# An attention-and-MLP block on one Trainium2 core: jumps over the general path moved to the ends of the instruction queues, and the first loads reordered

## Chip, cores, metric

One core of a Trainium2 chip runs the whole program. The metric is the device time of one execution in microseconds (us).

Names used below: PE is TensorE, DVE is VectorE, ACT is ScalarE, POOL is GpSimd, SP is SyncE, which in this kernel issues nearly all loads. A load's issue is the time that the engine spends on handing it to the DMA engines; it lands when the data have arrived. In listings "SPq" is SP's queue of DMA issues and "PEclk" the TensorE clock that the chip granted, as a share of full speed.

## The reference, cut to what matters

```python
mod = (silu(c) @ w_mod)                      # 6 blocks of 640: sa, ca, ga, sb, cb, gb
h = layernorm(x) * (1 + ca) + sa             # x: 2048 x 640
q = h @ wq                                   # 32 heads of 128
p = softmax(q @ k_cache.T * 128 ** -0.5)     # 2048 x 2048 for each head
x = x + ga * ((p @ v_cache) @ wo)
... # second half: layernorm, two small matrices with gelu and shifts, an MLP of 1728
```

The kernel goes through the heads in groups of four and through the 2048 query rows in four chunks of 512. A "step" is one head of one chunk. Step 0 is head 0 of chunk 0, steps 1 to 3 are heads 1 to 3 of chunk 0, and step 4 is head 0 of chunk 1. So in the first 50 us the kernel has to fetch the modulation weights, the query weights and the keys and values of four heads, while it already computes.

## The kernel before

The kernel records its operations with priorities; a list scheduler then fixes the order on each engine's queue. The general path, code that the usual input does not take, lies in the program between two parts of each queue. `FIRST` says after how many operations each engine jumps over it, and `HINT` where it announces the jump.

```python
    ENG = ("PE", "ACT", "DVE", "POOL", "SP")
    FIRST = {"PE": 3, "ACT": 10000, "DVE": 0, "POOL": 7, "SP": -5}
    HINT = {"PE": 0, "ACT": -30, "DVE": 0, "POOL": 0, "SP": -12}
    ...
        for e, eng in names.items():
            n = self.HINT[e] % len(self.seq[e])
            run(e, 0, n)
            hint = eng.mark_branch_hint_location()
            run(e, n, self.FIRST[e])
            eng.br("fast").branch_hint(hint)
        es.close()
        general()
        nc.switch_bb("fast")
        for e, eng in names.items():
            run(e, self.FIRST[e], None)
```

The loads of the start. A number such as -296 is a priority, lower is earlier; `gate` makes a load wait for an earlier one; `need=from_slot(n)` holds it until the softmax of slot n has run. Keys are loaded with a transposing DMA in four chunks of 512 keys, and only SP issues those.

```python
    def load_k(h, prio, gate=(), need=()):
        b = h % NKV
        for i in range(4):
            dmaT(lambda e, i=i: e.dma_start_transpose(K_ap[b][:, i * 512:(i + 1) * 512]..., A_k_cache[0, h, i * 512:(i + 1) * 512, :]),
                 128, gate if i or h else (), (K[b][i],), prio + 0.01 * i, need)

    load_wq(0, 0, 1, -297)                                # query weights of head 0
    load_k(0, -296, gate=(wm[2],))
    ln1(0, -280)                                          # layernorm of chunk 0
    ...
    dma("ACT", lambda e: e.dma_start(pre_ap, mod_src(2)), 800, (wm[1],), pre_t, -292)   # modulation block 2, 800 KB
    ...
    load_v(0, -290, "ACT", gate=(wm[1],))                 # head 0's values, 512 KB

    def load_head(h):
        first = step_of(h // HG, 0, h % HG)
        pr = (first - 12) * NP if h >= HG else -310 + 20 * h
        n = first * NP - 14 if h < HG else (first - 12) * NP
        load_k(h, pr, (wm[2],) if h == 1 else (), from_slot(n))
        load_v(h, pr + 1, gate=(wm[2],) if h == 1 else (), need=from_slot(n + 1))
    ...
    load_wq(0, 1, HG, -295.985, gate=(wm[2],))            # query weights of heads 1 to 3, 480 KB
```

Chunk 1's rows are normalised on DVE and then turned by four transposing DMAs, also issued by SP; DVE applies the modulation to the result. That gives `hT` of chunk 1, which step 4 needs.

Of the kernel before, what the change touches and what calls it, by code (L numbers as in the profile page):

```python
# [6 lines left out]
ACT = mybir.ActivationFunctionType  # L7
# [33 lines left out]
class Plan:  # L41
# [1 line left out]


    ENG = ("PE", "ACT", "DVE", "POOL", "SP")
    FIRST = {"PE": 3, "ACT": 10000, "DVE": 0, "POOL": 7, "SP": -5}
    HINT = {"PE": 0, "ACT": -30, "DVE": 0, "POOL": 0, "SP": -12}

    def __init__(self):
        self.ops = []  # L50
# [113 lines left out]
    def emit(self, nc, es, ndma, redo, flag, general):  # L164
# [82 lines left out]
# [6 lines that stand above are left out]
# [3 lines left out]
        for e, eng in names.items():  # L256
            run(e, self.FIRST[e], None)
            eng.wait_ge(self.flag_op.sem, self.flag_op.semval)
# [7 lines left out]
def fast_path(nc, es, flag, A_x, A_k_cache, A_v_cache, A_wq, A_wo, B_w1, B_w2, B_w3, B_w4, c, w_mod, out):  # L266
# [9 lines left out]
    HG = 4  # L276
# [57 lines left out]
    K = [[T() for _ in range(4)] for _ in range(NKV)]  # L334
# [14 lines left out]
    hT = [[T() for _ in range(KT)] for _ in range(NC)]  # L349
# [11 lines left out]
    xn = [T(t[:]) for t in xn_t]  # L361
# [18 lines left out]
    from_slot = lambda n: () if n < 0 else (lambda: exps[n],)  # L380

    def dma(eng, fn, kb, reads, writes, prio, need=(), after=()):
        return P.op(eng, fn, {"SP": 480, "ACT": 480, "POOL": 1000}[eng], reads, writes, prio, dma=True, kb=kb, need=need, after=after)
# [31 lines left out]
    wm = [T() for _ in range(KT)]  # L415
# [38 lines left out]
    saT, caT = T(small(KT)), T(small(KT))  # L454
# [9 lines left out]
    mvs = [[T() for _ in range(4)] for _ in range(NMV)]  # L464
    rs_ap = [small(4) for _ in range(NMV)]
    rs = [T() for _ in range(NMV)]
# [45 lines left out]
    def normed(dst, dst_t, src, src_t, g, i, fp, prio):  # L512
        P.op("DVE", lambda e: e.tensor_scalar(out=dst, in0=src, scalar1=mv_ap[g][:, i, 0:1], scalar2=rs_ap[g][:, i:i + 1],
                                              op0=ALU.subtract, op1=ALU.mult),
             430 if fp else 240, (src_t, mvs[g][i], rs[g]), (dst_t,), prio)

    COST = {"POOL": (1600, 950), "DVE": (825, 430)}

    def tt(eng, out, a, b, op, rd, wr, prio):
        P.op(eng, lambda e: e.tensor_tensor(out=out, in0=a, in1=b, op=op), COST[eng][0], rd, wr, prio, lat=300 if eng == "POOL" else None)  # L520
# [11 lines left out]
                 (src_t, rs[g], mvs[g][i]), (out_t,), prio)  # L532


    XP, XS = (0, -294, -20, -20), (0, -1, 22, 44)

    def ln1(ch, prio):
        g = ln_slot()
        xs = x0 if ch == 0 else load_x2(4 * ch, XP[ch], from_slot(XS[ch])) + load_x2(4 * ch + 2, XP[ch], from_slot(XS[ch]))
        for a, z in ((0, 2), (2, 4)) if ch < 2 else ((0, 4),):  # L540
            for i in range(a, z):
                ln_stats(xs[i].ap, (xs[i],), g, i, prio, 0.0 if ch == 0 else 2000.0)
            if ch == 0:
                rstd_act(g, a, z, prio - 100)
            else:
                rstd_dve(g, a, z, prio - 1)
            for i in range(a, z):
                normed(xn[i].ap, xn[i], xs[i].ap, xs[i], g, i, False, prio - 1)
        raw = [T() for _ in range(4)]
        if ch == 0:  # L550
            hq = Tile(pool="S0")
            hp = [Tile(pool="O0"), Tile(pool="O1"), hq, hq, Tile(pool="M")]

            def hslice(k, i0, i1):
                return hp[k].ap.bitcast(BF16)[:, (1024 if k == 3 else 0) + i0 * 128:(1024 if k == 3 else 0) + i1 * 128]
            for i in range(4):
                def tr(e, i=i):
                    for k in range(KT):
                        ins = e.transpose(hslice(k, i, i + 1), xn[i][:, k * 128:(k + 1) * 128], ident_t[:])
                    return ins  # L560
                P.op("PE", tr, 330, (xn[i], ident), (hp[0], hp[1], hq, hp[4]), (-286.6 if i < 2 else -280) + 0.1 * i, accum=True)
            for k in (0, 2, 4, 1, 3):
                if k % 2:
                    P.op("ACT", lambda e, k=k: e.activation(hT_t[0][:, k, :], hslice(k, 0, 4), ACT.Identity,
                                                            scale=caT[:, k:k + 1], bias=saT[:, k:k + 1]),
                         770, (hp[k], saT, caT), (hT[0][k],), -280 + k)
                else:
                    P.op("DVE", lambda e, k=k: e.tensor_scalar(out=hT_t[0][:, k, :], in0=hslice(k, 0, 4), scalar1=caT[:, k:k + 1],  # L568
                                                               scalar2=saT[:, k:k + 1], op0=ALU.mult, op1=ALU.add),
                         540, (hp[k], saT, caT), (hT[0][k],), -280 + k)  # L570
        else:
            for i in range(4):
                dmaT(lambda e, i=i: e.dma_start_transpose(hT_t[ch][:, :, i * 128:(i + 1) * 128], xn[i].ap), 160, (xn[i],), (raw[i],), prio - 400)  # L573
            for k in range(KT):
                P.op("DVE", lambda e, k=k: e.tensor_scalar(out=hT_t[ch][:, k, :], in0=hT_t[ch][:, k, :], scalar1=caT[:, k:k + 1],  # L575
                                                           scalar2=saT[:, k:k + 1], op0=ALU.mult, op1=ALU.add),
                     210, tuple(raw) + (saT, caT), (hT[ch][k],), prio)


    def load_k(h, prio, gate=(), need=()):  # L580
        b = h % NKV
        for i in range(4):
            dmaT(lambda e, i=i: e.dma_start_transpose(K_ap[b][:, i * 512:(i + 1) * 512].unsqueeze(1), A_k_cache[0, h, i * 512:(i + 1) * 512, :]),
                 128, gate if i or h else (), (K[b][i],), prio + 0.01 * i, need)

    def load_v(h, prio, eng="SP", gate=(), need=()):
        b = h % NKV
        dma(eng, lambda e: e.dma_start(V_ap[b][:, :, 0:128], A_v_cache[0, h].rearrange("(t p) d -> p t d", p=128)), 512, gate, (V[b],), prio, need)

    def load_wq(g, a, b, prio, need=(), gate=()):  # L590
        dma("SP", lambda e: e.dma_start(wq_t[g % 2][:, :, a * 128:b * 128],
                                        A_wq[:, (g * HG + a) * 128:(g * HG + b) * 128].rearrange("(k p) d -> p k d", p=128)),
            160 * (b - a), gate, tuple(wq[g % 2][a:b]), prio, need)
# [4 lines left out]

    step_of = lambda g, ch, hh: (g * NC + ch) * HG + hh
    of_step = lambda s: (s // (NC * HG), s // HG % NC, s % HG)  # L600
    load_wq(0, 0, 1, -297)
    load_k(0, -296, gate=(wm[2],))
    ln1(0, -280)


    def modulation(p, hf, w_ap, w_t, pool, key, prio):
        m = Tile(pool=pool)
        sl = slice(hf * HD, (hf + 1) * HD)
        for k in range(KT):
            P.op("PE", lambda e, k=k: e.matmul(m[:, 0:HD], s_bc[:, k, :], w_ap[:, k, sl], start=(k == 0), stop=(k == KT - 1)),  # L610
                 MM(HD), (s_bc,) + w_t, (m,), key(k), accum=True)
        P.op("DVE", lambda e: e.tensor_scalar_add(out=mod[p][hf].ap, in0=m[:, 0:HD], scalar1=1.0 if p == 4 else 0.0),
             490, (m,), (mod[p][hf],), prio)

    mod_src = lambda p: w_mod[:, p * D:(p + 1) * D].rearrange("(k p) n -> p k n", p=128)
    pre_ap = KV_t[:, (NKV - 1) * KVW:(NKV - 1) * KVW + KT * D].rearrange("p (k n) -> p k n", k=KT)
    pre_t = tuple(K[NKV - 1]) + (V[NKV - 1],)
    dma("ACT", lambda e: e.dma_start(pre_ap, mod_src(2)), 800, (wm[1],), pre_t, -292)
    for hf in range(2):
        modulation(2, hf, pre_ap, pre_t, "O%d" % hf, lambda k, hf=hf: (-262, 0.5)[hf] + 0.01 * k, -50)  # L620
    v_ones(NKV - 1)
    load_v(0, -290, "ACT", gate=(wm[1],))

    def load_head(h):
        first = step_of(h // HG, 0, h % HG)
        pr = (first - 12) * NP if h >= HG else -310 + 20 * h
        n = first * NP - 14 if h < HG else (first - 12) * NP
        load_k(h, pr, (wm[2],) if h == 1 else (), from_slot(n))
        load_v(h, pr + 1, gate=(wm[2],) if h == 1 else (), need=from_slot(n + 1))

    def load_group(g):
        if g:
            load_wq(g, 0, HG, (step_of(g, 0, 0) - 8) * NP, from_slot((step_of(g, 0, 0) - 8) * NP))
        load_wo(g, (step_of(g, 0, 0) - 2) * NP, from_slot((step_of(g, 0, 0) + 1) * NP + 12 * (g == 0)))

    load_wq(0, 1, HG, -295.985, gate=(wm[2],))
    for h in range(1, NKV):
        load_head(h)
    load_group(0)
# [3 lines left out]
    for n, p in enumerate((4, 3, 5)):  # L643
        dma("SP", lambda e, n=n, p=p: e.dma_start(w_half[n % 2], mod_src(p)), 800, (), (W12[n % 2],) + (w2b if n == 1 else ()) + tuple(wm),
            MS * NP - 30 + n, from_slot((MS + 2 * n) * NP - 20))
        for hf in range(2):
            modulation(p, hf, w_half[n % 2], (W12[n % 2],) + (w2b if n == 1 else ()), "M",
                       lambda k, i=2 * n + hf: NP * (MS + i) + 4.65 + k, NP * MS - 60)

    TAIL = ("A0 B0 B1 A1 B2 B3 WO B4 B5 I3 A2 B6 C0 B7 D0 D1 D2 B8 D3 B9 C1 D4 A3 B10 B11 "  # L650
            "B12 D5 B13 D6 B14 D7 B15 C2 D8 D9 D10 D11 C3 D12 D13 D14 D15").split()
    WOKEY = 3000 + 50 * TAIL.index("WO")
    QUAD = (2, 3)
    WOD, CH, I3D = -100, -1000, -200


    evac, last_ot = [], []
# [156 lines left out]
    for s in range(NS):  # L814
# [3 lines left out]
        g, ch, hh = of_step(s)  # L818
# [138 lines left out]
    pr = 3400  # L957
# [762 lines left out]
```

## Time and profile before

| | before |
|---|---|
| median of 3 runs | 1390.7 us (1390.07 to 1392.28) |
| span of the profiled run | 1391.3 us |
| PE busy | 1379.4 us, 99% |
| ACT, DVE busy | 79%, 39% |

The first lines of the page of the kernel before: engines with busy time and share, and in the last line the chain of waits that ended last, by engine.

```profile
span 1391.3 us, 29861 instructions
PE 1379.4 (99%) x13128; PEld 941.2 (68%) x13128; DVE 539.6 (39%) x1401; ACT 1101.5 (79%) x1143; POOL 100.9 (7%) x88
...
PE 97%; DVE 1%; DMA 1%; SPq 0%; issue 0%; ACT 0%
```

PE is the limit; the change touches no arithmetic, so it can only win or lose PE's few gaps. These are the gaps of the start, from PE's timeline of the kernel before (start, duration, engine, line, operation, output<-inputs, size, count, and in brackets the idle time before it and what ended it):

```profile
11.74 0.29 PE L448 MATMUL f_M<-f_s_bf,f_W 128*128 128x1 bf16 x6
13.38 0.25 PE L448 MATMUL f_M<-f_s_bf,f_W 128*128 128x1 bf16 x4 [1.34 <-issue]
...
14.85 2.34 PE L666 MATMUL f_M<-f_hT,f_wq 128*128 128x512 bf16 x5 [0.64 <-DVE f_hT L568]
...
45.55 1.25 PE L666 MATMUL f_M<-f_hT,f_wq 128*128 128x512 bf16 x4 [0.26 <-DVE f_hT L575]
46.64 0.59 PE L734 MATMUL f_S<-f_PQ,f_KV 128*128 128x512 bf16 x2
49.17 0.61 PE L753 MATMUL f_O<-f_KV,f_PQ 128*128 128x129 bf16 x8 [1.94 <-DMA f_KV<-in_A_v_cache_dram]
```

Three things are to be seen. A group of ten small matmuls is cut in two by 1.34 us in which PE waits for nothing that is recorded ("issue"). The first query projection (line 666) takes 2.34 us for five matmuls, where the one at 45.55 takes 1.25 for four: it ran at about half clock (PEclk was 0.50 from 14.48 to 17.89). And at 49.17 PE waits 1.94 us for the values of head 3.

SP's queue in the same run says when the loads went out. A duration here is the time that SP spent on the issues, not the transfer:

```profile
10.70 0.58 SPq L591 DMA_DIRECT2D f_wq<-in_A_wq_dram  x1
11.32 4.52 SPq L583 DMA_TRANSPOSE f_KV<-in_A_k_cache_dram  x2
...
36.99 6.01 SPq L573 DMA_TRANSPOSE f_hT<-f_xn  x4
43.04 1.26 SPq L583 DMA_TRANSPOSE f_KV<-in_A_k_cache_dram  x1
44.35 0.58 SPq L588 DMA_DIRECT2D f_KV<-in_A_v_cache_dram  x1
```

Line 591 is the query weights of heads 1 to 3, line 573 the transposes of chunk 1, the last line head 3's values. When each load landed is read from the last of the events that raise its semaphore: the query weights at 19.17, chunk 1's last transpose at 44.41, head 3's values at 49.04. One key load of head 0, taken alone from the same queue, matters later:

```profile
9.53 1.12 SPq L583 DMA_TRANSPOSE f_KV<-in_A_k_cache_dram  x1
```

### The profile page before, as it was taken

Reading aid. Unit: us, or ns where it says so; the run is one execution under the profiler, and the core shown is the slowest. Engines: PE = TensorE matmul, PEld = TensorE weight load, DVE = VectorE, ACT = ScalarE, POOL = GpSimd, SP = SyncE. Lnnn points to the kernel's source line nnn. Section 1 sums busy time; section 2 is a strip of 40 time slices with the busy share of each in tenths; the row PEclk is TensorE's granted clock in tenths of the full one; section 3 lists DMA queues with packets and bytes.
Section 4 is the critical chain, followed back from the end, with each engine's and each line's share of the span. In section 5 each row is a group of like instructions: output and inputs, shape, how many; then the busy total and the mean of one; then the engine's idle time right before and its main releaser. Section 6 shows DMA issues by size and latency. Waiting matters only on the chain.

```text
span 1391.3 us, 29861 instructions
## 1 busy us (share of the span) xinstructions
PE 1379.4 (99%) x13128; PEld 941.2 (68%) x13128; DVE 539.6 (39%) x1401; ACT 1101.5 (79%) x1143; POOL 100.9 (7%) x88
## 2 busy tenths in 40 slices
PE   9999999999999999999999999999999999999999
PEld 6667767777777777777777776777776766645554
DVE  5453232333233322333233323332333245987553
ACT  5888888888888898888888888888888888732222
POOL 0000000000000000000000000000333248200000
PEclk9999999999999999999999999999999999999999
DMA  9651623161214221241205122612254102531210
GB/s 220 130 115 31 117 78 83 36 107 35 46 36 84 58 46 36 48 92 30 54 17 98 31 45 36 107 36 46 55 91 114 17 16 48 120 53 24 53 43 25
DMA packets 259179, 88.90 MB, mean 64 GB/s; under 512 B 236705, under 2 KB 257762, under 8 KB 259042
## 3 DMA queue, kind: packets, MB, share of 16 engines
q1 hardware_dynamic: 255762, 84.59, 30.7%
q10 hardware_dynamic: 3280, 2.33, 0.7%
q8 instruction: 105, 1.72, 0.5%
q14 instruction: 32, 0.26, 0.1%
HBM read 43.48 MB, written 2.62 MB: 33 GB/s over the span
## 4 chain that ended last, share of the span: by engine, by line
PE 97%; DVE 1%; DMA 1%; SPq 0%; issue 0%; ACT 0%
PE f_O L753 33%; PE f_S L734 31%; PE f_M L666 10%; PE f_M L691 10%; PE f_M L928 3%; PE f_S L914 2%; PE f_O L914 2%; PE f_S L928 2%; PE f_S L887 1%; PE f_S L864 1%; PE f_O L864 1%; PE f_M L887 1%; DMA f_W<-in_w_mod_dram 0%; DMA f_KV<-in_A_v_cache_dram 0%; SPq L573 0%; PE f_M L610 0%
## 5 line engine op out<-in xcount | busy, mean ns | idle before, releaser
L736 ACT ACTIVATE f_PQ<-f_S 128x1024 bf16<-128x1024 f32 x1024 | 1041.0, 1023 | 148.2 <-PE f_S L734 135.1
L753 PEld LDWEIGHTS f_O<-f_KV,f_PQ 128*128 128x128 bf16 x8192 | 589.4, 98 | 233.7 <-issue 2.4
L734 PE MATMUL f_S<-f_PQ,f_KV 128*128 128x512 bf16 x2048 | 726.9, 379 | 0.2 <-ACT f_PQ L736 0.2
L753 PE MATMUL f_O<-f_KV,f_PQ 128*128 128x129 bf16 x8192 | 713.0, 220 | 2.7 <-DMA f_KV<-in_A_v_cache_dram 1.9
L699 DVE TENSOR_TENSOR f_y<-f_M,f_y 128x320 f32<-128x320 f32 x192 | 94.3, 491 | 536.3 <-PE f_M L691 536.3
L691 PE MATMUL f_M<-f_wo,f_OO 128*128 128x320 bf16 x992 | 272.9, 299 | 0.0
L734 PEld LDWEIGHTS f_S<-f_PQ,f_KV 128*128 128x128 bf16 x2048 | 196.7, 97 | 30.5 <-ACT f_PQ L736 1.2
L666 PE MATMUL f_M<-f_hT,f_wq 128*128 128x512 bf16 x640 | 177.3, 381 | 1.1 <-DVE f_hT L568 0.6
L691 PEld LDWEIGHTS f_M<-f_wo,f_OO 128*128 128x128 bf16 x992 | 96.1, 98 | 28.5
L762 DVE TENSOR_TENSOR f_OO<-f_O,f_rl 128x256 bf16<-128x256 f32 x256 | 108.4, 423 | 8.1
L669 DVE CAST f_PQ<-f_M 128x512 bf16<-128x512 f32 x128 | 88.5, 691 | 56.9 <-PE f_M L666 56.8
L520 POOL TENSOR_TENSOR f_y<-f_y,f_mod 128x640 f32<-128x640 f32 x32 | 49.6, 1560 | 820.1 <-DVE f_y L699 819.9
L666 PEld LDWEIGHTS f_M<-f_hT,f_wq 128*128 128x128 bf16 x640 | 62.2, 98 | 65.9 <-DVE f_hT L575 1.5
L760 DVE RECIPROCAL f_rl<-f_O 128x2 f32<-128x2 f32 x256 | 43.4, 169 | 32.1 <-PE f_O L753 27.9
L928 PE MATMUL f_M<-f_KV,f_OO 128*128 128x320 bf16 (+1 forms) x308 | 47.1, 300 | 0.0
L917 ACT ACTIVATE f_OO<-f_O 128x512 bf16<-128x512 f32 (+1 forms) x28 | 16.6, 596 | 38.5 <-PE f_O L914 38.5
L526 ACT ACTIVATE f_xn<-f_y,f_small 128x640 bf16<-128x640 f32 x10 | 9.1, 915 | 41.6 <-DVE f_small L505 41.6
L928 PEld LDWEIGHTS f_M<-f_KV,f_OO 128*128 128x128 bf16 (+1 forms) x308 | 28.6, 97 | 18.7 <-issue 7.0
L697 DVE COPY f_y<-f_M 128x320 f32<-128x320 f32 x32 | 15.7, 490 | 63.5 <-PE f_M L691 63.5
L481 DVE BATCH_NORM_STATS2 f_small<-f_y 128x6 f32<-128x320 f32 x64 | 29.6, 480 | 2.0 <-POOL f_y L520 2.0
L917 ACT ACTIVATE f_OO<-f_S 128x512 bf16<-128x512 f32 (+1 forms) x28 | 16.7, 595 | 13.1 <-PE f_S L914 13.1
L942 DVE TENSOR_TENSOR f_y<-f_M,f_y 128x640 f32<-128x640 f32 x10 | 8.2, 825 | 43.2 <-PE f_M L928 43.2
(134 smaller groups left out, 513.9 us busy)
## 6 DMA issues: line engine op xcount, KB each, us to landing
f_KV<-in_A_v_cache_dram SPq DMA_DIRECT2D x31, 512.0 KB, 4.8
f_wo<-in_A_wo_dram SPq DMA_DIRECT2D x8, 640.0 KB, 4.4
f_xin<-in_A_x_dram SPq DMA_DIRECT2D x15, 320.0 KB, 4.6
f_wq<-in_A_wq_dram SPq DMA_DIRECT2D x7, 640.0 KB, 4.6
f_W<-in_w_mod_dram SPq DMA_DIRECT2D x3, 800.0 KB, 4.9
out_dram<-f_xin SPq DMA_DIRECT2D x15, 160.0 KB, 1.8
f_KV<-in_B_w_dram SPq DMA_DIRECT2D x5, 432.0 KB, 3.3
f_KV<-in_A_k_cache_dram SPq DMA_TRANSPOSE x128, 2.7
```

The costliest lines, as they stand in the source:

```text
L520: P.op(eng, lambda e: e.tensor_tensor(out=out, in0=a, in1=b, op=op), COST[eng][0], rd, wr, prio, lat=300 if eng == "POOL" else None)
L666: P.op("PE", lambda e, i=i, kk=kk: e.matmul(m.ap, wq_t[g % 2][:, kk, hh * 128:(hh + 1) * 128], hT_t[ch][:, kk, :], start=(i == 0), stop=(i ...
L669: P.op("DVE", lambda e: e.tensor_copy(q.ap, m.ap), 690, (m,), (q,), s * NP - 90)
L691: P.op("PE", lambda e, m=m, qt=qt, hf=hf, hh=hh: e.matmul(m[:, 0:HD], OT_ap[gs][:, qt, hh, :], wo_t[g % 2][:, hh, hf * HD:(hf + 1) * HD], ...
L699: P.op("DVE", lambda e, m=m, yt=yt: e.tensor_tensor(out=yt.ap, in0=m[:, 0:HD], in1=yt.ap, op=ALU.add), 490, (m, yt), (yt,), s * NP - 60)
L734: P.op("PE", lambda e, sp=sp, r=r, kt=kt: e.matmul(sp[:, r * QC:(r + 1) * QC], K_ap[b][:, kt * 128:(kt + 1) * 128], q.ap, start=True, stop ...
L736: x = P.op("ACT", lambda e, sp=sp, pt=pt: e.activation(pt.ap.rearrange("p k q -> p (k q)"), sp.ap, ACT.Exp, scale=SCALE), 1021, (sp,), (pt ...
L753: ins = e.matmul(o[bk][:, w * 129:w * 129 + 129], pt[:, r, qt * 128:(qt + 1) * 128], V_ap[b][:, u, 0:129], start=(u == 0 and w == 0), stop ...
L760: P.op("DVE", lambda e, ov=ov, i0=i0: e.reciprocal(rl_t[:, i0:i0 + 2].unsqueeze(2), ov[:, 0:258].rearrange("p (u d) -> p u d", u=2)[:, :, ...
L762: evac.append(P.op("DVE", lambda e, ov=ov, i0=i0, bk=bk: e.tensor_tensor(out=On_ap[gs][:, 2 * bk:2 * bk + 2, hh, :], in0=ov[:, 0:258].rear ...
L914: P.op("PE", lambda e, m=m, f=f, kk=kk, fs=fs: e.matmul(m[0:fs, :], w3_ap[:, kk, f * 128:f * 128 + fs], nT_ap[ch][:, kk, :], start=(kk == ...
L928: P.op("PE", lambda e, f=f, hf=hf, fs=fs: e.matmul(m[:, hf * 512:hf * 512 + HD], gT_ap[0:fs, f, i * 128:(i + 1) * 128], w4_ap[f][0:fs, hf ...
```

## The change

Read from the diff, the change aims at PE's gap at 12 us, by letting no engine jump early, and at PE's wait for head 3's values, by loading the values of heads 1 to 3 in one batch.

```diff
-    FIRST = {"PE": 3, "ACT": 10000, "DVE": 0, "POOL": 7, "SP": -5}
-    HINT = {"PE": 0, "ACT": -30, "DVE": 0, "POOL": 0, "SP": -12}
+    FIRST = {"PE": 100000, "ACT": 100000, "DVE": -6, "POOL": 100000, "SP": -5}
+    HINT = {"PE": -300, "ACT": -30, "DVE": -60, "POOL": -1, "SP": -12}
 ... (four cost estimates of the scheduler, and a later priority for normalising chunk 0)
-    XP, XS = (0, -294, -20, -20), (0, -1, 22, 44)
+    XP, XS = (0, -294.5, -20, -20), (0, -1, 22, 44)
 ... in load_k
-                 128, gate if i or h else (), (K[b][i],), prio + 0.01 * i, need)
+                 128, gate if i or h else (), (K[b][i],), prio + (1.6 if h == 0 and i else 0) + 0.01 * i, need)
 ...
-    load_wq(0, 0, 1, -297)
-    load_k(0, -296, gate=(wm[2],))
+    load_wq(0, 0, 1, -298)
+    load_k(0, -297.5, gate=(wm[2],))
 ...
-    dma("ACT", lambda e: e.dma_start(pre_ap, mod_src(2)), 800, (wm[1],), pre_t, -292)
+    dma("SP", lambda e: e.dma_start(pre_ap, mod_src(2)), 800, (wm[2],), pre_t, -297)
     for hf in range(2):
-        modulation(2, hf, ..., lambda k, hf=hf: (-262, 0.5)[hf] + 0.01 * k, -50)
+        modulation(2, hf, ..., lambda k, hf=hf: 0.5 + hf + 0.01 * k, -50)
-    load_v(0, -290, "ACT", gate=(wm[1],))
+    load_v(0, -296.5, gate=(wm[2],))
 ... in load_head
+        if h in (1, 2, 3):
+            load_k(h, (-294, -290, -289)[h - 1], (wm[2],), () if h < 3 else from_slot(n))
+            load_v(h, (-293, -291, -290.5)[h - 1], gate=(wm[2],))
+            return
 ...
-    load_wq(0, 1, HG, -295.985, gate=(wm[2],))
+    load_wq(0, 1, HG, -295.5, gate=(wm[2],))
 ... (order of the tail: B9 before D3, A3 before D4; WOD -200, I3D 100)
```

In effect: PE's and POOL's jumps come at the end and DVE's before its last six operations; modulation block 2 and head 0's values are issued by SP, not by ACT; the query weights of heads 1 to 3 go behind all of head 0's keys; the values of heads 1 to 3 go in one batch before head 2's keys.

More of the change, by code (lines that the diff above doesn't have):

```diff
@@ L514, in normed @@
                                               op0=ALU.subtract, op1=ALU.mult),
-             430 if fp else 240, (src_t, mvs[g][i], rs[g]), (dst_t,), prio)
-    COST = {"POOL": (1600, 950), "DVE": (825, 430)}
+             445, (src_t, mvs[g][i], rs[g]), (dst_t,), prio)
+    COST = {"POOL": (1600, 950), "DVE": (825, 590)}
     def tt(eng, out, a, b, op, rd, wr, prio):
@@ L547, in ln1 @@
             for i in range(a, z):
-                normed(xn[i].ap, xn[i], xs[i].ap, xs[i], g, i, False, prio - 1)
+                normed(xn[i].ap, xn[i], xs[i].ap, xs[i], g, i, False, prio - 1 if ch else prio + 0.5)
         raw = [T() for _ in range(4)]
@@ L576, in ln1 @@
                                                            scalar2=saT[:, k:k + 1], op0=ALU.mult, op1=ALU.add),
-                     210, tuple(raw) + (saT, caT), (hT[ch][k],), prio)
+                     400, tuple(raw) + (saT, caT), (hT[ch][k],), prio)
     def load_k(h, prio, gate=(), need=()):
@@ L617, in fast_path @@
     pre_t = tuple(K[NKV - 1]) + (V[NKV - 1],)
-    dma("ACT", lambda e: e.dma_start(pre_ap, mod_src(2)), 800, (wm[1],), pre_t, -292)
+    dma("SP", lambda e: e.dma_start(pre_ap, mod_src(2)), 800, (wm[2],), pre_t, -297)
     for hf in range(2):
-        modulation(2, hf, pre_ap, pre_t, "O%d" % hf, lambda k, hf=hf: (-262, 0.5)[hf] + 0.01 * k, -50)
+        modulation(2, hf, pre_ap, pre_t, "O%d" % hf, lambda k, hf=hf: 0.5 + hf + 0.01 * k, -50)
     v_ones(NKV - 1)
-    load_v(0, -290, "ACT", gate=(wm[1],))
+    load_v(0, -296.5, gate=(wm[2],))
     def load_head(h):
@@ L627, in load_head @@
         n = first * NP - 14 if h < HG else (first - 12) * NP
-        load_k(h, pr, (wm[2],) if h == 1 else (), from_slot(n))
-        load_v(h, pr + 1, gate=(wm[2],) if h == 1 else (), need=from_slot(n + 1))
+        if h in (1, 2, 3):
+            load_k(h, (-294, -290, -289)[h - 1], (wm[2],), () if h < 3 else from_slot(n))
+            load_v(h, (-293, -291, -290.5)[h - 1], gate=(wm[2],))
+            return
+        load_k(h, pr, need=from_slot(n))
+        load_v(h, pr + 1, need=from_slot(n + 1))
     def load_group(g):
@@ L648, in fast_path @@
                        lambda k, i=2 * n + hf: NP * (MS + i) + 4.65 + k, NP * MS - 60)
-    TAIL = ("A0 B0 B1 A1 B2 B3 WO B4 B5 I3 A2 B6 C0 B7 D0 D1 D2 B8 D3 B9 C1 D4 A3 B10 B11 "
+    TAIL = ("A0 B0 B1 A1 B2 B3 WO B4 B5 I3 A2 B6 C0 B7 D0 D1 D2 B8 B9 D3 C1 A3 B10 B11 D4 "
             "B12 D5 B13 D6 B14 D7 B15 C2 D8 D9 D10 D11 C3 D12 D13 D14 D15").split()
@@ L653, in fast_path @@
     QUAD = (2, 3)
-    WOD, CH, I3D = -100, -1000, -200
+    WOD, CH, I3D = -200, -1000, 100
     evac, last_ot = [], []
```

## The prediction

> **What bounds the kernel.** TensorE: the page has PE busy 99% of 1391.3 us, the chain of waits is 97% PE; ACT is at 79%, DVE at 39%. From 60 to 1150 us the PE timeline has no such gap, and the change adds and removes no arithmetic: it can only touch PE's few gaps. From the PE timeline (start to start, less the usual pitch):
> - 1.3 us at 12.03, inside a group of ten matmuls, waiting for nothing ("issue" in the chain);
> - 0.6 us at 45-46, q projection of step 4, for the second chunk's hT (last row transpose landed 44.4, then DVE);
> - 1.9 us at 49.17, for head 3's values, which the SP queue issued only at 44.35 (landed 49.04);
> - 2.3 us at 1227-1230, for DVE to evacuate the last output projection.
>
> **What the change does.**
> 1. Jumps. PE, DVE and POOL jumped over the general path at their queues' start; now at the end. The jump is cheap (PE's branch 0.34 us, under a wait for w_mod). The Trainium skill ("Runtime: NRT & Kernel Launch", Instruction fetch mechanics) says instructions come in blocks of 256 and a taken branch breaks sequential prefetch. About 200 instructions after PE's jump comes the 12.03 gap[...]. Straight-line PE should lose it: -1.3 us, perhaps -0.6 more, because three projection matmuls after it ran at half rate (0.43 us against 0.21). At the end the jumps lie in waits (DVE idles 1.7 us before its last six operations).
> 2. Loads. ACT no longer issues the third modulation block and head 0's values; SP does, after w_mod's third block (landed 9.5). Two modulation groups move behind the first scores and no longer hide the q copy: +0.5 us. Values of heads 1 to 3 go in one batch before head 2's keys; the 1.9 us wait goes. But each value load held the DMA about 3 us (head 1's landed 28.7, the keys before it 25.6), so head 2's keys and the second chunk's transposes behind them come 1 to 4 us later (estimate from these landings). Step 2 wants keys at 33-34 (landed 30.6-32.9), step 4 wants hT at 44. So part of the gain should return as waits for keys near 34 or, chiefly, hT near 44-48.
> 3. Tail. DVE's order around the output projection is the same, so the 2.3 us stay. A3 is pulled ahead of D4; its input has about 3 us of slack left. About 0, risk +1.
>
> **Sum.** Start -1.3 (-1.9 with the clock), modulation +0.5, values -1.9 to -2.5, hT/keys given back +0.5 to +3, tail 0: about -2.4 us.
>
> **Prediction: 1388.3 us, 8 in 10 between 1385.0 and 1391.2.** Faster by over 2%: 0.01; within 2%: 0.98; slower by over 2%: 0.01 (2% is 28 us; all gaps together are under 12).
>
> **What would show it.** No "issue" gap near 12; first q projection about 1.3 us before 14.85; no PE wait on values at 49; instead waits on DVE f_hT (or f_KV keys) between 33 and 49, over 0.6; output projection gaps and steady pitch unchanged; end no longer.
>
> **What would make it wrong.** An instruction stall that only moves (another engine near the end, PE at a later block); a late wq load for heads 1-3 (needed about 19, landed 19.2 before); value loads blocking SP until hT comes after 49 (slower than before); hT in time after all (1386).

## The result

| | before | after |
|---|---|---|
| median | 1391.49 us (1390.07 to 1392.29, 4 runs) | 1395.07 us (1393.54 to 1395.10, 4 runs) |
| ratio | 1 | 1.0024, 95% interval 1.0007 to 1.0042 |
| span of the profiled run | 1391.3 us | 1393.7 us |

Ratios here and below are the mean time of one kernel's runs over that of the other's of the same rounds, so they are not quite the ratio of the medians quoted beside them. The change made the kernel slower by about 3.3 us (1.0 to 5.8 by the interval): the class "within 2%" held, the number (1388.3) and its range (to 1391.2) did not.

The lines of the page of the changed kernel:

```profile
span 1393.7 us, 29855 instructions
PE 1379.2 (99%) x13128; PEld 941.9 (68%) x13128; DVE 540.5 (39%) x1401; ACT 1101.6 (79%) x1143; POOL 101.0 (7%) x88
...
PE 96%; DVE 1%; DMA 1%; SPq 1%; issue 0%; ACT 0%
```

The page says nearly nothing: PE's busy time is the same to 0.2 us, and the span is 2.4 us longer. The answer is in PE's timeline of the changed kernel:

```profile
12.10 0.39 PE L448 MATMUL f_M<-f_s_bf,f_W 128*128 128x1 bf16 x10
...
13.71 1.51 PE L670 MATMUL f_M<-f_hT,f_wq 128*128 128x512 bf16 x5 [0.64 <-DVE f_hT L568]
16.00 0.61 PE L738 MATMUL f_S<-f_PQ,f_KV 128*128 128x512 bf16 x2 [0.79 <-DVE f_PQ L673]
...
23.13 1.83 PE L670 MATMUL f_M<-f_hT,f_wq 128*128 128x512 bf16 x5 [4.30 <-DMA f_wq<-in_A_wq_dram]
24.75 1.06 PE L738 MATMUL f_S<-f_PQ,f_KV 128*128 128x512 bf16 x2
...
50.15 1.32 PE L670 MATMUL f_M<-f_hT,f_wq 128*128 128x512 bf16 x4 [0.26 <-DVE f_hT L575]
51.31 0.59 PE L738 MATMUL f_S<-f_PQ,f_KV 128*128 128x512 bf16 x2
```

The ten small matmuls are in one piece and the first query projection starts 1.14 us sooner (13.71 against 14.85). Then PE waits 0.79 us for DVE's copy of the first queries, and 4.30 us at 23.13 for the query weights of heads 1 to 3. Behind that wait the scores (line 738) take 1.06 us a pair instead of 0.59. The wait at 49.17 for head 3's values is gone, and a short wait for chunk 1 stands at 50.15.

SP's queue of the changed kernel shows where the weights were:

```profile
8.66 0.39 SPq L618 DMA_DIRECT2D f_KV<-in_w_mod_dram  x1
9.10 0.52 SPq L588 DMA_DIRECT2D f_KV<-in_A_v_cache_dram  x1
9.66 7.75 SPq L583 DMA_TRANSPOSE f_KV<-in_A_k_cache_dram  x3
17.46 0.58 SPq L591 DMA_DIRECT2D f_wq<-in_A_wq_dram  x1
...
26.25 4.59 SPq L588 DMA_DIRECT2D f_KV<-in_A_v_cache_dram  x3
30.89 11.41 SPq L583 DMA_TRANSPOSE f_KV<-in_A_k_cache_dram  x7
42.34 5.25 SPq L573 DMA_TRANSPOSE f_hT<-f_xn  x4
```

The chain of waits of the same run, cut to these microseconds, takes the three key loads apart and names what follows (start, duration, what):

```profile
9.66 5.14 SPq L583
...
14.84 1.27 SPq L583
...
17.46 5.62 DMA f_wq<-in_A_wq_dram
```

SP spent 5.14 us on the issue of one key load, right behind modulation block 2 and head 0's values; the next took 1.27. The modulation block landed at 14.32, half a microsecond before that issue ended. In the kernel before, where those two large loads went out by ACT, the same key load took 1.12 us (9.53 to 10.65). So the query weights went out at 17.46 instead of 10.70 and landed at 23.08 instead of 19.17.

Was it bandwidth? The busy times by stretches, first the kernel before, then the changed one (the last three columns are PEclk, the DMA engines' share and GB/s):

```profile
16.00:20.00 4.00, 4.00 (x18) 1.90 (x17) 1.68 (x3) 1.17 (x2) 0.13 (x1) 0.76 1.30 226
...
24.00:26.00 2.00, 2.00 (x27) 1.53 (x25) 1.87 (x7) 1.97 (x3) 0.00 (x0) 1.00 1.04 215
```

```profile
16.00:20.00 4.00, 2.83 (x16) 1.48 (x16) 0.98 (x2) 3.07 (x3) 0.13 (x1) 1.00 0.57 104
...
24.00:26.00 2.00, 2.00 (x9) 0.90 (x8) 1.00 (x2) 0.15 (x1) 0.00 (x0) 0.50 0.66 137
```

Just before the wait, at 16 to 20 us, the DMA engines of the changed kernel moved 104 GB/s where the kernel before moved 226. Up to 16 us both had moved as much (256 and 255 GB/s on average). So in this stretch the DMA engines lacked work; that SP's held entries were the reason is tested by runs 4, 11 and 12 below. And at 24 to 26 us PE had half the clock. (The DMA share adds up the time of packets and can pass 1.)

To place the whole loss, add up over all pairs of consecutive matmuls the time from start to start less the streaming time at full clock (0.21 us for 512 columns in undisturbed stretches, 0.025 for one column). The sums, in us, worked out from the traces:

| window, us | before | after | difference |
|---|---|---|---|
| 0 to 15 | 4.95 | 4.15 | -0.80 |
| 15 to 25 | 1.87 | 6.02 | +4.15 |
| 25 to 44 | 0.60 | 1.70 | +1.10 |
| 44 to 60 | 3.28 | 1.38 | -1.90 |
| 60 to 120 | 1.77 | 2.25 | +0.48 |
| sum | 12.47 | 15.50 | +3.03 |

From 120 to 1150 us the two agree to 0.03. One short wait of PE for DVE, late in the attention, stands at 1163.53 in the kernel before and at 1166.60 in the changed one: 3.07 us later, which the table accounts for. It serves below as a milestone. The +0.48 is one new wait of 0.47 us on DVE at 78.22; it stands in all seven traces with the value batch (the changed kernel, runs 2 to 5, 11 and 12) and in none of the seven without it, but how the batch delays DVE was not followed up. The spans differ by only 2.4 us. Most of the rest lies at 1220 to 1240 us, where PE's excess is 4.19 us before and 3.57 after: the profiled run of the kernel before had half clock from 1229.6 to 1233.0, that of the changed kernel had not.

A wait of PE that is told below without its line is measured in the same way, start to start; it comes out 0.14 to 0.17 us longer than the idle time that a line prints.

### The profile page after: what moved, and what is told of

Same layout as the page of the kernel before. It is cut to its first block, busy times and chain, and to the rows that moved or that the text cites. A ratio compares the mean times of both kernels' runs of the same rounds, so it can differ in the third digit from the quotient of the medians.

```text
span 1393.7 us, 29855 instructions
## 1 busy us (share of the span) xinstructions
PE 1379.2 (99%) x13128; PEld 941.9 (68%) x13128; DVE 540.5 (39%) x1401; ACT 1101.6 (79%) x1143; POOL 101.0 (7%) x88
## 4 chain that ended last, share of the span: by engine, by line
PE 96%; DVE 1%; DMA 1%; SPq 1%; issue 0%; ACT 0%
PE f_O L757 33%; PE f_S L738 31%; PE f_M L670 10%; PE f_M L695 10%; PE f_M L932 3%; PE f_S L918 2%; PE f_O L918 2%; PE f_S L932 2%; PE f_S L868 1%; PE f_S L891 1%; PE f_O L868 1%; SPq L583 1%; PE f_M L891 0%; DMA f_W<-in_w_mod_dram 0%; DMA f_wq<-in_A_wq_dram 0%; DMA f_wq<-f_xn 0%
## 5 line engine op out<-in xcount | busy, mean ns | idle before, releaser
L932 PE MATMUL f_M<-f_KV,f_OO 128*128 128x320 bf16 (+1 forms) x280 | 42.8, 300 | 0.0
L932 PE MATMUL f_S<-f_KV,f_OO 128*128 128x320 bf16 (+1 forms) x168 | 25.7, 300 | 0.0
```

The source lines that it names most:

```text
L932: P.op("PE", lambda e, f=f, hf=hf, fs=fs: e.matmul(m[:, hf * 512:hf * 512 + HD], gT_ap[0:fs, f, i * 128:(i + 1) * 128], w4_ap[f][0:fs, hf ...
```

## The experiments

Theory A: the gap at 12 us is an instruction fetch behind the early jump and costs what it seems to, but PE's first 50 us are paced by loads in SP's one queue. An earlier start then only lengthens the next wait for a load. The new order loses because SP holds the entry behind two large loads, so that the query weights come late, and because the value batch puts chunk 1's transposes late. Rivals: the jumps cost as much at the end as at the start; the DMA engines were short of bandwidth; the new tail order costs the time.

Kernels called "before" are runs of the kernel before on the same chip and in the same rounds: median 1390.88 (11 runs) beside the first four, 1391.56 (9 runs) beside the next four, 1392.32 (9 runs) beside the last four. All twelve kernels gave correct results.

### 1. The jumps alone

The kernel before with the two lines `FIRST` and `HINT` of the change.

```diff
-    FIRST = {"PE": 3, "ACT": 10000, "DVE": 0, "POOL": 7, "SP": -5}
-    HINT = {"PE": 0, "ACT": -30, "DVE": 0, "POOL": 0, "SP": -12}
+    FIRST = {"PE": 100000, "ACT": 100000, "DVE": -6, "POOL": 100000, "SP": -5}
+    HINT = {"PE": -300, "ACT": -30, "DVE": -60, "POOL": -1, "SP": -12}
```

> The kernel before with only the jump positions of the change. Theory A (instruction fetch, absorbed): the gap of 1.3 us at 12 is gone and the first q projection starts at about 13.5 instead of 14.85, but head 3's values still land at about 49 because the SP queue, not PE, sets that time; so PE's wait there grows from 1.9 to about 3.3 us and the time stays within 0.5 us of before. Rival (my prediction's sum): the gain at 12 comes through to the end, 1.3 to 1.9 us faster than before. A third outcome, slower by over 0.5 us, would put part of the loss on the jumps.

Measured: 1391.71 us (1389.31 to 1395.55, 6 runs), ratio 1.0003 (0.9990 to 1.0016). PE's timeline of this run:

```profile
13.29 1.06 PE L666 MATMUL f_M<-f_hT,f_wq 128*128 128x512 bf16 x4 [1.09 <-DVE f_hT L568]
...
18.41 1.25 PE L666 MATMUL f_M<-f_hT,f_wq 128*128 128x512 bf16 x5 [0.95 <-DMA f_wq<-in_A_wq_dram]
...
48.08 0.62 PE L753 MATMUL f_O<-f_KV,f_PQ 128*128 128x129 bf16 x8 [2.40 <-DMA f_KV<-in_A_v_cache_dram]
```

The gap is gone. This trace lacks some matmul records, the first of this projection among them; by its weight load at 12.83 the projection starts 2.02 us sooner. Then a wait for the query weights appears, and the wait for head 3's values grows from 1.94 to 2.40 us (they landed at 47.95, 1.1 us sooner than before). ACT's exponentials, whose records are complete, show what was left of the gain: they run 1.85 us ahead of the kernel before up to 43 us and 1.09 us ahead behind the wait for head 3's values. At 54 us they are 0.56 us behind, since the clock was halved from 49.14 to 52.55 (the third column from the end is PEclk):

```profile
50.00:51.00 1.00, 1.00 (x7) 0.63 (x6) 0.00 (x0) 0.43 (x2) 0.00 (x0) 0.50 1.04 350
```

So the waits for loads took up about half of the gain, as theory A says, and the half clock behind the last of them took the rest and more. Whether that stretch comes in every run is not known: the two runs whose mean clock was 1.000 took 1389.31 and 1389.85 us, below the fastest of before (1390.24). The six runs spread over 6 us, and the interval leaves room for a gain of 1.4 us.

### 2. The loads alone

The changed kernel with the old `FIRST` and `HINT` (the diff of 1, reversed).

> The changed kernel with the old jump positions (loads, priorities and tail as changed). If the loss is the loads' alone: the wq wait of step 1's q projection still ends at about 23 (wq landing fixed by the SP queue), the fetch gap at 12 is back and is absorbed by that wait, and the time is that of the changed kernel (about 1395, 3 to 4 us over before). If the jumps carry part of the loss: 1391 to 1393. If the fetch gain counts in full: 1396 to 1397.

Measured: 1395.55 us (1394.16 to 1398.5, 5 runs), ratio 1.0032 (1.0019 to 1.0045). The gap is back (1.41 us at 13.27). The query weights landed at 22.77, but the wait for them is only 0.56 us, since PE came later (the clock was at half from 14.6 to 21.4 us). Chunk 1's last transpose landed at 49.67, and PE waited 2.70 and 0.43 us for it. The loss of the change comes with the rest of it, and no cost of the jumps at the ends is seen. The rest is the loads, the tail (run 5) and the scheduler's cost estimates, which no run tries alone.

### 3. Query weights ahead of the keys

In the changed kernel:

```diff
-    load_wq(0, 1, HG, -295.5, gate=(wm[2],))
+    load_wq(0, 1, HG, -296.2, gate=(wm[2],))
```

> The changed kernel with one load moved: the wq load of heads 1 to 3 is issued right after head 0's values, before the three key transposes (chunks 1 to 3 of head 0). Theory A (the SP queue is blocked: the first of these transposes held the queue 5.14 us, so wq was issued at 17.46): wq is issued at about 9.7 and lands at 18 to 19; PE's wait for wq falls from 4.3 us to under 1; some wait for the keys may come in its place (0 to 1.5 us); end 3 to 5 us under the changed kernel unless hT at 49 or a later load takes it back (hT is issued by the same queue, so part is likely given back: 1 to 5 us). Rival B (the DMA engines have no bandwidth left): wq lands at 21 or later, since only about 1.9 us of keys' time is taken from in front of it, and the wait is still over 2 us.

Measured: 1397.35 us (1396.67 to 1398.46, 5 runs), ratio 1.0044 (1.0031 to 1.0057). My expectation of a gain missed. The weights landed at 18.44 and their wait went, but now their own issue was held 4.22 us (10.29 to 14.51), so it is the entry behind the two large loads that is held, a plain load as well as a transposing one. The keys behind it came late instead. PE's timeline:

```profile
19.06 0.59 PE L738 MATMUL f_S<-f_PQ,f_KV 128*128 128x512 bf16 x2 [1.19 <-DMA f_KV<-in_A_k_cache_dram]
...
50.65 1.68 PE L670 MATMUL f_M<-f_hT,f_wq 128*128 128x512 bf16 x3 [3.00 <-DVE f_hT L575]
```

Chunk 1's last transpose landed at 50.16. So there is a second limit behind the first: taking the wait at 23 us away only brought PE sooner to the wait for chunk 1.

### 4. The two large loads back on ACT

```diff
-    dma("SP", lambda e: e.dma_start(pre_ap, mod_src(2)), 800, (wm[2],), pre_t, -297)
+    dma("ACT", lambda e: e.dma_start(pre_ap, mod_src(2)), 800, (wm[1],), pre_t, -292)
-    load_v(0, -296.5, gate=(wm[2],))
+    load_v(0, -290, "ACT", gate=(wm[1],))
```

> The changed kernel with the third modulation block and head 0's values issued by ACT after w_mod's second block, as before; the rest of SP's order as changed. Theory A: the key transposes no longer stand behind 1.3 MB in their own queue, so wq is issued at 14 to 15.5 instead of 17.46 and PE's wait for it falls to 0.5 to 2.5 us. Rival B (bandwidth): the same bytes are ahead of wq, it lands at about 23 again and the wait stays at 4 us.

Measured: 1393.65 us (1390.66 to 1395.37, 5 runs), ratio 1.0023 (1.0010 to 1.0036); the profiled run was the fastest. From its SP queue:

```profile
8.70 4.43 SPq L583 DMA_TRANSPOSE f_KV<-in_A_k_cache_dram  x3
13.17 0.58 SPq L591 DMA_DIRECT2D f_wq<-in_A_wq_dram  x1
```

The second key load's issue, the first of these three, took 1.13 us, the query weights went out at 13.17 and landed at 19.96, PE waited 2.36 us for them, chunk 1 landed at 45.11 and cost no wait. So the hold goes when the two loads leave SP's queue. In this trace the milestone is at 1162.70, 0.83 us sooner than in the kernel before. But the runs vary by 5 us, and what the profiled run escaped in the others is not known, so the time decides little.

### 5. The old tail

The changed kernel with the old order of the tail and the old `WOD` and `I3D`.

```diff
-    TAIL = ("A0 ... D1 D2 B8 B9 D3 C1 A3 B10 B11 D4 "
+    TAIL = ("A0 ... D1 D2 B8 D3 B9 C1 D4 A3 B10 B11 "
-    WOD, CH, I3D = -200, -1000, 100
+    WOD, CH, I3D = -100, -1000, -200
```

> The changed kernel with the tail's order and priorities as before. Expected: the same as the changed kernel within 1 us (1394 to 1396), the 2.3 us at the output projection in both. If the tail's reorder is worth something, it is slower or faster by over 1 us.

Measured: 1393.96 us (1392.94 to 1394.65, 4 runs), ratio 1.0017 (1.0002 to 1.0032). The ratio lies within the interval of the changed kernel's 1.0024. The waits of 1.6 and 0.7 us at the last output projection stand in every kernel. The tail is worth nothing that these runs can see.

### 6. The values not in one batch

```diff
-            load_v(h, (-293, -291, -290.5)[h - 1], gate=(wm[2],))
+            load_v(h, (-293, -289.5, -288.5)[h - 1], gate=(wm[2],), need=() if h < 3 else from_slot(n + 1))
```

> The changed kernel with the batch of values taken apart again (head 2's values after head 2's keys, head 3's after the second chunk's transposes, as before); the late wq load stays. Theory A2 (two waits in series in one blocked SP queue; either alone costs the time): hT lands 2 to 4 us earlier than the 49.0 of the changed kernel, but PE still waits about 4 us for wq at 19-23 and reaches step 4's projection only at about 49, where it then waits little; the end is within 1.5 us of the changed kernel (1393.5 to 1396). Rival (the batch of values alone is the loss): back to before, 1391.

Measured: 1392.93 us (1392.32 to 1394.66, 5 runs), ratio 1.0013 (1.0000 to 1.0027): a little better than expected, but by time not told apart from the changed kernel (1.0007 to 1.0042); its milestone is 1.45 us sooner. The wait for the query weights is nearly the same (4.29 us at 22.93, 4.46 in the changed kernel, with half clock behind both), the transposes of chunk 1 were issued from 39.42 instead of 42.34 and landed at 46.03 instead of 49.01, with no wait for them or for head 3's values. The value batch is what made chunk 1 late.

### 7. Both 3 and 6

> Both at once: values apart again and wq before the three key transposes. Theory A2: wq wait and hT wait both shrink; PE's waits up to 52 us sum to what before had (about 5 us with the fetch gap gone), and the time is 1390 to 1392.5, that of before. It should beat both of its halves (wq alone 1397.4, values alone about 1395) by over 2 us, which no theory of one cause gives. If hT still lands at 48 or later, the SP queue is late for another reason (modulation block and head 0's values in SP's own queue) and the time is 1393 to 1396.

Measured: 1393.43 us (1391.73 to 1394.69, 5 runs), ratio 1.0011 (0.9997 to 1.0025). That is not the expected gain over 6. The wait for the query weights went (landed 18.06), and PE got to 50.09 sooner, where it waited 2.81 us for head 3's values (landed 49.95). That is the wait of the kernel before, once more.

### 8. The jumps at the ends, and head 3's values by ACT

The kernel before with the jumps of the change; head 3's values are issued by ACT, and the last two key chunks of head 3 wait until chunk 1 has been transposed:

```diff
 ... the two lines of 1, and in load_k and load_head:
-                 128, gate if i or h else (), (K[b][i],), prio + 0.01 * i, need)
+                 128, gate if i or h else (), (K[b][i],), prio + 0.01 * i, from_slot(15) if h == 3 and i > 1 else need)
+        if h == 3:
+            load_v(h, 16.5, "ACT", need=from_slot(16))
+            return
         load_v(h, pr + 1, ...)
```

> A try for a better kernel: the kernel before with the jumps at the ends, head 3's values issued by ACT after the 17th exp (so not behind SP's transposes), and the last two key chunks of head 3 after the second chunk's hT transposes. Theory: the waits at 44 (hT, 1.1 us) and 48 (head 3's values, 2.6 us) of the jumps-only run fall under 0.5 us each; ACT pays about 0.5 us for the issue, in steps where it is as busy as PE; 1387.5 to 1389.5, 2 to 3 us under before. Rival: the DMA engines, not the queue, set when these land, so the waits only move to the keys of head 3 and the time stays at 1391.

Measured: 1387.77 us (1386.8 to 1389.24, 5 runs), ratio 0.9973 (0.9959 to 0.9986): faster than both kernels. Head 3's values landed at 39.74 and chunk 1 at 42.30, and there is no wait over 0.5 us between 25 and 60 us. Two things were changed beside the jumps, the queue of the values and the hold on the keys; which of them counts was not tested.

### 9 and 10. The same again, and the same with the early jumps

Run 9 is the kernel of run 8 again, as the neighbour of run 10, which puts the two lines `FIRST` and `HINT` back to those of the kernel before.

> The kernel that beat both (the kernel before with its jumps at the ends, head 3's values issued by ACT and the last two of head 3's key loads held until chunk 1 has been transposed), once more, as the neighbour of the next run. Both theories: 1386.5 to 1389.5, 0.996 to 0.999 of the kernel before; no wait of TensorE over 0.5 us between 40 and 50 us.

> The same with the jumps back at the starts of the queues. Theory (the instruction fetch costs about 1.3 us at 12 us, and its removal showed nothing in the change only because a later wait for a load took it up): with the waits for head 3's values and chunk 1's transposes gone there is nothing to take it up, so this run is 1.0 to 1.6 us slower than its neighbour, about 1388.8 to 1389.5; the gap of 1.3 to 1.4 us inside the ten-matmul group is back, no wait over 0.5 us at 40 to 50 us. Rival (moving the jumps is worth nothing, whatever the loads do): within 0.4 us of its neighbour.

Measured: 1387.16 us (1387.07 to 1388.12, 5 runs), ratio 0.9962 (0.9949 to 0.9976), with the jumps at the ends; 1390.0 us (1388.75 to 1390.57, 5 runs), ratio 0.9978 (0.9964 to 0.9992), with the early jumps. The slowest of run 9's runs is faster than the fastest of run 10's. By the medians the jumps are worth 2.84 us here, 2.39 by the means, where no gain was seen in run 1. So the gain is real here. The size that I expected (1.0 to 1.6) was too small, and part of it is the clock: all of run 9's runs have a mean clock of 1.000, and the one run of run 10 that has it took 1388.75 us, 1.59 over run 9's median. Run 8, the same kernel as run 9 on another chip, had the ratio 0.9973, only 0.0005 below run 10's. First SP's queue and PE's timeline of run 9, then of run 10:

```profile
1.63 1.40 SPq L417 DMA_DIRECT2D f_W<-in_w_mod_dram  x3
```

```profile
12.51 1.51 PE L669 MATMUL f_M<-f_hT,f_wq 128*128 128x512 bf16 x5 [0.64 <-DVE f_hT L568]
```

```profile
1.63 2.58 SPq L417 DMA_DIRECT2D f_W<-in_w_mod_dram  x3
```

```profile
8.43 0.18 PE L448 MATMUL f_M<-f_s_bf,f_W 128*128 128x1 bf16 x1 [0.49 <-DMA f_W<-in_w_mod_dram]
...
13.23 0.25 PE L448 MATMUL f_M<-f_s_bf,f_W 128*128 128x1 bf16 x4 [0.71 <-issue]
...
14.71 1.93 PE L669 MATMUL f_M<-f_hT,f_wq 128*128 128x512 bf16 x5 [0.64 <-DVE f_hT L568]
```

With the early jumps the gap has only 0.71 us in this run, but two costs came beside it that I had not counted. SP's issues of the modulation weights took 2.58 instead of 1.40 us, so that the last of them landed at 10.19 instead of 9.16. And the granted clock at 16 to 18 us was 0.50 instead of 1.00. The first projection starts 2.20 us later, and the milestone of the late attention lies 2.71 us later (1161.36 against 1158.65).

### 11. The query weights issued by ACT

In the changed kernel:

```diff
-    load_wq(0, 1, HG, -295.5, gate=(wm[2],))
+    load_wq(0, 1, HG, -295.5, gate=(wm[2],), eng="ACT")
```

> The changed kernel with only the query weights of heads 1 to 3 issued by ACT instead of SP. Theory (those weights came late because SP held its next loads behind modulation block 2 and head 0's values, not because the DMA engines lacked bandwidth): they are issued at about 10 to 12 us and land at 17 to 20, TensorE's wait of 4.3 us at 23 us falls under 1 us; the rest of SP's queue moves up a little, chunk 1's transposes land at 47 to 49 and still cost about 0.5 to 1 us, so the gain is 1 to 3 us: 1391.5 to 1394. Rival (the bytes ahead of them set the landing): they land at 22 to 23 whichever queue issues them and the wait stays over 3 us, time within 0.7 us of the changed kernel's 1395.

Measured: 1398.16 us (1397.26 to 1399.6, 5 runs), ratio 1.0039 (1.0026 to 1.0053). The first half of the theory held: the weights were issued at 8.16, landed at 15.46, and the wait at 23 us is gone. So it was not bandwidth. The second half failed. From the chain of waits:

```profile
9.16 6.51 SPq L583
```

With three large loads under way the second key load was held 6.51 us. What stood behind it in SP's queue gained little and lost it again: head 1's keys went out at 19.46 (21.15 in the changed kernel), the values at 25.78 (26.25), but chunk 1's transposes only at 43.61 (42.34). The waits are 0.94 us for keys at 18.19, 1.87 for values at 30.55, 2.20 for keys at 36.98 and 4.13 for chunk 1 at 51.70 (landed 51.21).

### 12. Head 0's values behind the query weights

In the changed kernel:

```diff
-    load_v(0, -296.5, gate=(wm[2],))
+    load_v(0, -295.2, gate=(wm[2],))
```

> The changed kernel with head 0's values (512 KB) issued behind the query weights instead of ahead of the keys. Theory (the entry behind two large loads is held until the first of them is nearly through; how long depends on what is outstanding): with only modulation block 2 ahead, the second key load is held less, under 3 us where it was 5.1, the weights are issued at 12 to 15 us instead of 17.5 and land at 18 to 21, TensorE's wait at 23 us falls from 4.3 to under 1.5 us; head 0's values land at about 22 to 24 and may cost a new wait before the first output product. Time 1392.5 to 1395.5. Rival (a transposed load waits until every plain load ahead has landed): the second key load is still released only when modulation block 2 has landed, at about 14.3, so it is held over 4 us, and the weights gain at most 1 us.

Measured: 1395.51 us (1394.89 to 1396.78, 5 runs), ratio 1.0023 (1.0009 to 1.0037), at the upper edge of what I expected. SP's queue of this run:

```profile
8.27 0.39 SPq L618 DMA_DIRECT2D f_KV<-in_w_mod_dram  x1
8.70 4.35 SPq L583 DMA_TRANSPOSE f_KV<-in_A_k_cache_dram  x3
13.10 0.58 SPq L591 DMA_DIRECT2D f_wq<-in_A_wq_dram  x1
```

All three key loads took 4.35 us together, the first of them 1.20, though modulation block 2 landed only at 13.72: behind one large load the next entry was hardly held, behind two it is. The rival (a transposing load waits for every plain load ahead) is out. And PE's timeline:

```profile
17.41 1.24 PE L670 MATMUL f_M<-f_hT,f_wq 128*128 128x512 bf16 x5
...
48.53 2.53 PE L670 MATMUL f_M<-f_hT,f_wq 128*128 128x512 bf16 x5 [2.78 <-DVE f_hT L575]
```

The query weights (landed 17.33) cost no wait at all, PE was 5.7 us ahead of the changed kernel there, and when the projection of chunk 1 began only 1.0 of it was left (48.53 against 49.51), after waits of 0.87, 0.83, 1.98 and 2.95 us (start to start, less the usual pitch). The end was the same as the changed kernel's.

### What the twelve say together

The sums of PE's excess over the usual pitch, in us, for the traces with a full set of matmul records, and the milestone of the late attention:

| kernel | 0-15 | 15-25 | 25-44 | 44-60 | 60-120 | milestone |
|---|---|---|---|---|---|---|
| before | 4.95 | 1.87 | 0.60 | 3.28 | 1.77 | 1163.53 |
| after | 4.15 | 6.02 | 1.70 | 1.38 | 2.25 | 1166.60 |
| 6, values not batched | 4.12 | 5.91 | 1.64 | 0.64 | 1.79 | 1165.15 |
| 7, and weights ahead | 3.97 | 1.78 | 1.94 | 5.53 | 1.80 | 1166.09 |
| 12, V0 behind weights | 3.86 | 1.11 | 3.29 | 4.83 | 2.25 | 1166.43 |
| 11, weights by ACT | 3.17 | 2.49 | 4.52 | 6.42 | 2.23 | 1170.04 |
| 9, V3 by ACT | 3.24 | 1.43 | 0.56 | 0.79 | 1.76 | 1158.65 |
| 10, V3 by ACT, early jumps | 4.80 | 2.13 | 0.59 | 1.06 | 1.75 | 1161.36 |

Read 6, 7 and 12 against "after": what one column loses, another gains. The same for the jumps, in ratios to the kernel before:

| loads | early jumps | jumps at the ends |
|---|---|---|
| as before | 1 | 1.0003 (run 1) |
| as in the change | 1.0032 (run 2) | 1.0024 (the changed kernel) |
| V3 by ACT | 0.9978 (run 10) | 0.9962 (run 9) |

Each ratio is uncertain by 0.0013 or more, so a gain from the jumps is clear of noise only in the last row, where run 9 and run 10 had the same chip and rounds. That it is smaller where late loads wait fits the traces; the times alone do not show it.

## Why the prediction was wrong

1. *"Straight-line PE should lose it: -1.3 us, perhaps -0.6 more."* The effect was right, and its mechanism fits. The Trainium skill ("Runtime: NRT & Kernel Launch", section "Instruction fetch mechanics") says that instructions are fetched in blocks of 256 and that a taken branch breaks the sequential prefetch. The traces agree as far as they go. In all three kernels with early jumps (before, runs 2 and 10) the gap comes at the same place in PE's stream, 228 instruction records behind PE's branch, and a transfer of 16,384 bytes of instructions ends at 12.02, 11.94 and 11.80 us, 1.33 to 1.43 us before PE goes on; none of the eleven kernels with late jumps has the gap. But these have a like transfer too (at 10.01 in the changed kernel, 11.66 in run 9), so that PE waited for an instruction fetch is argued and not shown. (A passage of the prediction about the start of that fetch is cut: the transfer nearest to the gap starts at 10.90 us, over 1 us ahead of it.) The change really started its first projection 1.14 us sooner. But as a term of a sum the step was wrong: in the change the gain was taken up by the next load, in run 1 by waits for loads and by the half clock behind them.
2. *"+0.5 us"* for the modulation groups moved away from the query copy: it was 0.79 us idle, 0.95 by pitch.
3. *"The 1.9 us wait goes"*: it went.
4. *"hT/keys given back +0.5 to +3"*: in the changed kernel itself the waits for chunk 1 near 50 us sum to 0.88 us, against 0.6 in the kernel before. No wait for keys near 34 came. The range held, but only since PE was already late. The transposes landed 4.6 us later than before (49.01 against 44.41), just above the 1 to 4 that I had estimated.
5. The step that failed is item 2 of the prediction, "Loads", with its sum. It has no term for the query weights of heads 1 to 3. I had seen that they were needed about 19 us and landed at 19.2, and named them only under what would make the prediction wrong. They landed at 23.08 and PE waited 4.30 us, and half the clock behind it made most of the +1.10 at 25 to 44 us. What I had not asked is what SP does when two large loads move into its queue: I costed the move as a transfer ("about 3 us" a value load), but it is the issue that stops, 5.14 us against 1.12.
6. The sum itself was the wrong form. *"Start -1.3 ..., values -1.9 to -2.5, hT/keys given back ..."* adds gains of waits that lie one behind the other in one queue. Runs 1, 3, 7 and 12 each take one wait away, and the next one grows. In the change there are two limits, the query weights and chunk 1; run 12 removes the first and ends at the same time, run 6 removes the second and gains 1.45 us by the milestone, and run 11 takes the weights out of the queue and loses more behind it. Run 7 removes both and meets the old wait for head 3's values. What did win (runs 8 and 9) starts from the order of the kernel before, takes out of SP's queue the one large load that PE waited for last, and holds two key loads back.
7. *"Tail ... About 0"*: held (run 5).

What stays open: why a queue holds an entry behind two large loads (only that it does is shown); why the early jumps lengthen the issue of the modulation weights at 2 us (in all three kernels it ends 0.37 to 0.38 us behind a transfer of 16,384 bytes of instructions that begins at 1.95 to 1.98 us, which the late jumps do not have; that is a hint, not a proof); and why runs 1 and 4 spread over 5 to 6 us. The clock is part of such a spread: of the 29 runs of the kernel before in the experiments, the 12 with a mean clock of 0.997 or 0.998 took 1392.7 us on average, the 17 with 0.999 or 1.000 took 1391.0.

## What to carry to other kernels

Where several loads in one queue pace the start, do not add up the waits: find which load would be late next if the first wait went, and only count the gain up to there. Before moving a large load into a queue, look at how long the entries behind large loads take to issue there, and which small urgent load will stand behind them. A change that shows nothing, as the jumps did alone, can be worth keeping once the wait behind it is gone: the ratio was 1.0003 (0.9990 to 1.0016) for the jumps alone, and they won 2.84 us by the medians, part of it by the clock, with head 3's values on another queue and two key loads held.

## What the Trainium skill lacked or had wrong

- "DMA: Bandwidth & Descriptors", section "Issuing engines are not separate DMA queues", says that issuing from several engines only saves the sequencer's time to initiate the DMA, "which is usually small relative to the DMA itself". Here that time was not small: a key load behind two large loads took 5.14 us to issue (6.51 with a third under way) against 1.12 to 1.20 for the same load behind none or one; further down the queue of the kernel before, key loads behind one value load took 2.40 and 2.81 us. Issuing the two large loads from ACT saved that hold (1.13 us, run 4), and one value load from ACT was part of what won 0.4% (run 9).
- No page that I found says that the entry behind two large loads in a queue is held until about when the first of them has landed (held to 14.80, landed 14.32 in the changed kernel; 14.51 and 14.74 in run 3), whether it is a transposing load (5.14 us) or a plain one (4.22 us, run 3). The nearest is the timeline of a DMA issue in "Perfetto Trace Analysis", whose descriptor buffer can fill up; it gives no size and does not speak of earlier loads.
- "Runtime: NRT & Kernel Launch", section "Instruction fetch mechanics", names the stall at the branch. Here a gap came 228 instruction records later (1.34 us at 12 us, the branch itself cost 0.34 us under another wait), and early jumps came with a second cost that it does not name: SP's second issue of modulation weights took 1.16 to 1.78 us in all three kernels with early jumps and 0.43 in the eleven others.
- "TensorE: Matmul & The Clock Gate", section "What's actually happening", says that the clock falls to half after an idle window of about 3.4 us, free-running. The traces agree with the halving (0.50 at 24 to 26 us behind the wait of 4.30 us) and with the length (the stretches at half clock near the start last 3.41 or 6.83 us by the clock records), and its being a matter of phase fits them. But gaps well under that were enough at times: PEclk was 0.50 behind waits of 2.40 (run 1) and 2.78 us (run 12) and behind gaps of 1.34 and 0.64 us close together (kernel before, 15 to 17 us), and 1.00 behind 1.94 us (kernel before, 49 to 51 us).
